# Moving the inverse transforms and norm of the next row block into the h stage, with block 0 by pairs and two VectorE orders changed

## The chip, the cores and the metric

The kernel runs on one core of one Trainium2 chip. The metric is the device time in microseconds (us), taken over several runs. One run of each kernel was also profiled; the span of a profile is the time from its first to its last instruction and is about 2 us shorter than the same run's time. Engines are named as in the profile: PE is TensorE, PEld its weight loads, DVE VectorE, ACT ScalarE, POOL GpSimd, SP SyncE. The granted clock is the share of TensorE's full clock that the profile records, 1.00 at full speed. L851 is a line of the kernel; the changed kernel has other line numbers than the one before for the same operation (the transposed input's product h is L833 before and L851 after, the row products og L858 and L878, the w2T scaling L619 and L622).

## The reference, cut to what matters

The reference is the forward pass of a block with spectral mixing and an MLP, and all its gradients.

```python
sa, ca, ga, sb, cb, gb = silu(c) @ w_mod                # six rows of 512
h = layernorm(x) * (1 + ca) + sa
x = x + ga * irfft2(rfft2(h) * (w_r + 1j * w_i))        # 2048 x 512
h = layernorm(x) * (1 + cb) + sb
x = x + gb * (relu(h @ w1 + b1) ** 2 @ w2 + b2)         # F = 1792
...
out = x;  gradients of x, w_r, w_i, w1, b1, w2, b2, c, w_mod
```

The 2048 rows are 16 tiles of 128, in four row blocks of four tiles (b = 0 to 3, TB = 4, NB = 4). Every row block passes through the following stages:

- **g**: the last part of the inverse transform (psT, psY), the unfolding of y, x = x + ga y, and the norm n2rows.
- **h2r and h2T**: n2rows times (1 + cb) plus sb, written to DRAM, and read back transposed (blocks 1 to 3); block 0 is transposed on TensorE.
- **h**: h2T times w1, the relu and square, and gh, the gradient there.
- **o**: the output rows, h times w2.
- **gn**: the gradient rows, gh times w1T, and the gradient of the norm.

After the four blocks come grad_w1 beside the gradient's transforms, and grad_w2 beside the last row products.

## The kernel before

The loop over the blocks, and where g of the next block stands:

```python
        merge(stage_g(0))
        merge(stage_t(0))
        ...
        for b in range(NB):
            again0, again = f1_again(UT) if b == NB - 1 else ([], [])
            stage_h(b, again0)
            ...
            if b < NB - 1:
                merge(stage_o(b), stage_g(b + 1) + [lambda: None] * 3)
                ...
                merge(stage_gn(b, UT), parts + [lambda: None])
```

`merge` interleaves two lists in program order; a scheduler then decides each engine's final order by its own estimates, and every engine works through its order. `tc.issue_after(i)` holds what follows behind instruction i in that order. The end of the norm in stage g, where the round trip of the next block's h input begins:

```python
            def norm(j):
                ...                                      # x, statistics, n2rows of rows j, j + 1
                h2r = rows.tile([P, 2, D], BF16, name="h2r", bufs=1)
                nc.vector.tensor_tensor(h2r, n2b[b][:, j:j + 2, :], ...CB1_B..., op=ALU.mult)
                nc.vector.tensor_tensor(h2r, h2r, ...SB_B..., op=ALU.add)
                nc.sync.dma_start(h2_dram[:, t:t + 2, :], h2r)
                if b > 0:
                    nc.sync.dma_start(h2T[b][:, j:j + 2]..., h2_dram[:, t:t + 2, :]..., transpose=True)
```

The two scalings of w2T, all ahead of the first statistics, and the h stage with its column sums flushed in one place:

```python
    for h in range(2):
        for dc in range(4):
            wh = w2T[:, dc, h * F2:(h + 1) * F2]
            nc.vector.tensor_scalar(wh, wh, gb2x[:, dc:dc + 1], None, op0=ALU.mult)
    ...
        late, late_f1 = Delayed(2), Delayed(4)           # column sums, delayed by two
    ...
        def stage_h(b, extra):
            ...
            for fc in range(0, NFC, 2):                  # seven pairs
                ...
                if fc == 4:
                    late.flush()
                if fc >= 2 and extra:
                    extra.pop(0)()
```

## Time and profile before

| | before |
|---|---|
| time | 457.75 us median of 3 runs (457.12 to 461.03) |
| span of the profile, mean granted clock | 455.1 us, 0.966 |
| PE, DVE, ACT busy | 408.5, 362.0, 251.0 us (90%, 80%, 55%) |

The page's second part cuts the span into 40 slices of about 11.4 us. Each digit is a share in tenths, and 9 is 90% or more:

```profile
PE   2589899999699999995999599999999979997996
...
PEclk9979999999889999997999889999999999999899
```

The dips of PE in the 11th slice (from 114 us), the 19th (205 us) and the 23rd (250 us) are the hand-over of block 0 and the borders before the h stages of blocks 2 and 3, and the clock falls with them. A sum over one stretch runs from the last h product of block 0 to the first grad_w1 product, and holds nearly all of blocks 0 to 3 but the start. The columns are length; busy us and count of PE, weight loads, DVE, ACT and POOL; granted clock, DMA share, GB/s:

```profile
140.00:305.10 165.10, 153.35 (x758) 67.47 (x756) 127.90 (x270) 83.95 (x150) 0.14 (x2) 0.96 0.75 194
```

TensorE has 758 matmuls there, is idle for 165.10 - 153.35 = 11.75 us, and runs at a mean clock of 0.96.

### The profile page before, as it was taken

To read this page: it belongs to the slowest core of one execution; us is meant where nothing else is said; L and a number is where in the kernel's file an instruction comes from. 1 tells how busy PE (TensorE), PEld (TensorE's weight loads), DVE (VectorE), ACT (ScalarE), POOL (GpSimd) and SP (SyncE) were. 2 spreads that over 40 slices of the span, in tenths; PEclk is the share of its full clock that TensorE was granted. 3 is DMA by queue.
4 is the path that set the end of the run, shared out by engine and by line. 5 is a ranking of instruction groups with operands and counts; after the bars stand their busy time and mean duration, and the time that the engine had idled before them with its cause. 6 is when DMAs were issued, how large, how long until landed. Compare 5 with 4: busy or idle time off the path is not lost.

```text
span 455.1 us, 7052 instructions
## 1 busy us (share of the span) xinstructions
PE 408.5 (90%) x2375; PEld 198.9 (44%) x2375; DVE 362.0 (80%) x864; ACT 251.0 (55%) x470; POOL 12.6 (3%) x64
## 2 busy tenths in 40 slices
PE   2589899999699999995999599999999979997996
PEld 0134455664344434442444234445555655443332
DVE  6379889987997487895679879891965995998996
ACT  4247877658874176355724376645453648364531
POOL 6011000000000000000000000000000000000000
PEclk9979999999889999997999889999999999999899
DMA  9995679998579359749933899598799559999995
GB/s 241 235 269 143 177 281 279 286 290 211 158 283 254 100 117 269 231 119 185 307 130 93 191 232 302 207 226 228 205 268 337 157 155 295 254 229 280 250 224 188
DMA packets 149738, 101.09 MB, mean 222 GB/s; under 512 B 98753, under 2 KB 135494, under 8 KB 149062
## 3 DMA queue, kind: packets, MB, share of 16 engines
q1 hardware_dynamic: 149138, 100.12, 81.8%
q10 hardware_dynamic: 564, 0.53, 0.4%
q8 instruction: 18, 0.29, 0.3%
q14 instruction: 18, 0.15, 0.1%
HBM read 35.44 MB, written 41.60 MB: 169 GB/s over the span
## 4 chain that ended last, share of the span: by engine, by line
PE 46%; DVE 29%; DMA 10%; SPq 5%; ACT 5%; issue 4%; POOL 1%; DVEq 0%; ACTq 0%; POOLq 0%
PE mm L833 11%; PE og L858 8%; PE mm L1053 7%; PE mm L684 6%; PE mm L1122 3%; PE psC L303 2%; PE psG L341 2%; DMA h2T<-h_dram 2%; DMA w2T<-in_B_w_dram 2%; DMA n<-n_dram 2%; DVE gab L687 2%; DVE l_st L784 2%; SPq L1117 2%; SPq L563 1%; DVE gm_junk L465 1%
## 5 line engine op out<-in xcount | busy, mean ns | idle before, releaser
L684 PE MATMUL mm<-gT,w2T 128*128 128x512 bf16 x224 | 60.1, 398 | 9.4 <-DVE gab L687 8.9
L833 PE MATMUL mm<-h2T,w 128*128 128x512 bf16 x224 | 59.8, 412 | 5.1 <-DMA h2T<-h_dram 4.5
L1122 PE MATMUL mm<-g_sb,hn 128*128 128x512 bf16 x224 | 51.7, 385 | 2.5 <-DVE gw L1125 2.5
L1053 PE MATMUL mm<-gab,h_sb 128*128 128x448 bf16 x256 | 51.7, 352 | 0.6 <-ACT gw L1057 0.6
L858 PE MATMUL og<-w1T,gab 128*128 128x512 bf16 x224 | 50.9, 379 | 0.4 <-DVE o L923 0.4
L858 PE MATMUL og<-w,h 128*128 128x512 bf16 x224 | 51.1, 379 | 0.0
L835 ACT ACTIVATE r<-mm,b1col 128x512 bf16<-128x512 f32 x56 | 37.7, 686 | 18.8 <-PE mm L833 13.9
L833 PEld LDWEIGHTS <-w 128*128 128x128 bf16 x224 | 22.7, 104 | 37.1 <-issue 18.6
L684 PEld LDWEIGHTS <-w2T 128*128 128x128 bf16 x224 | 21.7, 101 | 33.1 <-issue 16.0
L1053 PEld LDWEIGHTS <-h_sb 128*128 128x128 bf16 x256 | 24.7, 98 | 22.5 <-issue 2.1
L1122 PEld LDWEIGHTS <-hn 128*128 128x128 bf16 x224 | 21.3, 99 | 28.8 <-issue 5.4
L858 PEld LDWEIGHTS <-h 128*128 128x128 bf16 x224 | 21.8, 98 | 25.7
L858 PEld LDWEIGHTS <-gab 128*128 128x128 bf16 x224 | 21.5, 98 | 25.8 <-issue 0.8
L837 DVE TENSOR_TENSOR h<-r 128x1024 bf16<-128x1024 bf16 x28 | 19.3, 689 | 13.9 <-ACT r L835 13.8
L687 DVE CAST gab<-mm 128x512 bf16<-128x512 f32 x28 | 19.1, 681 | 4.8 <-PE mm L684 4.8
L689 ACT CAST gab<-mm 128x512 bf16<-128x512 f32 x28 | 16.5, 590 | 9.4 <-PE mm L684 9.2
L871 ACT CAST G<-og 128x512 bf16<-128x512 f32 x16 | 9.2, 578 | 22.5 <-PE og L858 22.5
L1202 ACT ACTIVATE gs<-gn,inv 128x512 bf16<-128x512 bf16 x16 | 11.4, 716 | 18.4 <-DVE gn L1200 18.4
L1057 ACT CAST gw<-mm 128x448 bf16<-128x448 f32 x16 | 8.7, 541 | 22.1 <-PE mm L1053 15.5
L372 ACT ACTIVATE Tsb<-psT 128x512 bf16<-128x512 f32 x32 | 18.5, 604 | 3.3 <-PE psT L370 3.3
L413 DVE TENSOR_TENSOR p<-Z,G 128x1028 bf16<-128x1028 bf16 x8 | 5.6, 696 | 17.6 <-ACT gw L1057 9.2
L465 DVE SCALAR_TENSOR_TENSOR gm_junk<-wmc,onef,gmbc 128x512 bf16<-128x512 bf16 x24 | 17.9, 745 | 1.9 <-DMA wmc<-in_w_mod_dram 1.0
(286 smaller groups left out, 749.1 us busy)
## 6 DMA issues: line engine op xcount, KB each, us to landing
h_dram<-h SPq DMA_DIRECT2D x28, 256.0 KB, 3.0
gh_dram<-gab SPq DMA_DIRECT2D x28, 256.0 KB, 3.1
w<-in_B_w_dram SPq DMA_DIRECT2D x2, 1792.0 KB, 8.4
wmc<-in_w_mod_dram SPq DMA_DIRECT2D x12, 256.0 KB, 4.9
out_dram<-gwm SPq DMA_DIRECT2D x12, 256.0 KB, 3.4
wz_dram<-Z SPq DMA_DIRECT2D x8, 258.0 KB, 2.3
xs_dram<-Xs SPq DMA_DIRECT2D x8, 258.0 KB, 4.6
Z<-wz_dram SPq DMA_DIRECT2D x8, 258.0 KB, 4.4
```

The lines of the kernel that those rows point to most:

```text
L372: nc.scalar.activation(Tsb, ps, AF.Copy, scale=EF_S)
L465: nc.vector.scalar_tensor_tensor(out=junk, in0=wmc[:, i, :], scalar=K["onef"], in1=gmbc, op0=ALU.mult, op1=ALU.mult, accum_out=self.gsc[:, ...
L684: nc.tensor.matmul(ps, lhsT=w2T[:, dc, fc * P:(fc + 1) * P], rhs=gT[b][:, :, dc, :], start=(dc == 0), stop=(dc == 3))
L687: nc.vector.tensor_copy(out=gaT[b][:, fc, :], in_=ps)
L689: nc.scalar.copy(out=gaT[b][:, fc, :], in_=ps)
L833: nc.tensor.matmul(ps, lhsT=w1[:, dc, (fc + i) * P:(fc + i + 1) * P], rhs=h2T[b][:, :, dc, :], start=(dc == 0), stop=(dc == 3))
L835: nc.scalar.activation(r[:, i, :], ps, AF.Relu, bias=b1col[:, fc + i:fc + i + 1])
L837: nc.vector.tensor_tensor(h2, r, r, op=ALU.mult)
L858: nc.tensor.matmul(ps, lhsT=lhs(fc), rhs=rhs[:, fc, :], start=(fc == 0), stop=(fc == NFC - 1))
L1053: nc.tensor.matmul(ps[:, 0:W4], lhsT=h2_sb[:, t, dc * P:(dc + 1) * P], rhs=ghn[t // 4][:, t % 4, fs], start=(t == 0), stop=(t == NT - 1))
L1122: nc.tensor.matmul(ps, lhsT=hns[fc][:, t, :], rhs=g_sb[:, t, :], start=(t == 0), stop=(t == NT - 1))
L1202: nc.scalar.activation(gs[:, i, :], gn[:, i, :], AF.Copy, scale=inv1[:, t + i:t + i + 1], accum_out=rr[:, i, 0:1])
```

## The change

The intent is that the next block's h input is ready when TensorE is, that block 0 hands over sooner, and that VectorE does not stand in front of data that have not landed. In the prediction and below, A is the w2T order, B is block 0 and C is the move of g. The diff, cut to its core:

```diff
-    for h in range(2):                                   # A
+    def scale_w2(h):
         for dc in range(4):
             ...
+    scale_w2(0)
     for q in range(4):
         ...                                              # statistics of row quarter q
+        if q == 1:
+            with tc.issue_after(stats.ins):
+                scale_w2(1)
 ...
+    with tc.issue_after(last.ins):                       # B: table load ahead of time
+        nc.scalar.activation(warm, K["eps"], AF.Sqrt)
 ...
         def stage_g(b):
             def norm(j):
                 ...
-                h2r = ...; nc.sync.dma_start(h2_dram ...); transposed read of h2T
+        def stage_m(b):                                   # the same lines, on their own
+            return [lambda j=j: one(j) for j in (0, 2)]
 ...
         def stage_t(b):                                   # B: by pairs of rows
-            four rounds by column chunk: 4 transposes, 1 copy of 128 x 512
+            two rounds by row pair: 8 transposes, 4 copies of 128 x 256
 ...
-        late, late_f1 = Delayed(2), Delayed(4)            # C: column sums later
+        late, late_f1 = Delayed(4), Delayed(4)
-                if fc == 4:
-                    late.flush()
+                if fc in (2, 6):
+                    late.pop(2)
 ...
+                with tc.issue_after(K["gh"]):             # f1 scalings behind gh
                     nc.vector.tensor_tensor(v, v, ...GA_B..., op=ALU.mult)
 ...
-        merge(stage_g(0))
-        merge(stage_t(0))
+        g0, t0 = stage_g(0), stage_t(0)
+        merge(g0[0:3] + t0[0:1] + g0[3:5] + t0[1:2])
 ...
-            stage_h(b, again0)                            # C: g beside h
+                m = stage_m(0) if b == 0 else []
+                stage_h(b, m + stage_g(b + 1), 2 if b == 0 else 6)
-                merge(stage_o(b), stage_g(b + 1) + [lambda: None] * 3)
+                merge(stage_o(b), stage_m(b + 1) + [lambda: None] * 2)
```

The last argument of `stage_h` is the pair of products beside which the extra work begins.

More of the change, by code (lines that the diff above doesn't have):

```diff
@@ L153, in build_cf @@
     nc.vector.tensor_single_scalar(v, v, 1023, op=ALU.bitwise_and)
-    nc.scalar.activation(Cf, v, AF.Sin, scale=TWO_PI / 1024, bias=K["npi"])
+    last = nc.scalar.activation(Cf, v, AF.Sin, scale=TWO_PI / 1024, bias=K["npi"])
     nc.vector.tensor_scalar(Cf[:, 0:2, :], Cf[:, 0:2, :], efc[:, 2:3], None, op0=ALU.mult)
     K["Cf"] = Cf
+    warm = cpool.tile([P, 1], FP32, name="warm")
+    with tc.issue_after(last.ins):
+        nc.scalar.activation(warm, K["eps"], AF.Sqrt)
 def iotas_lf(tc, g):
@@ L626 @@
             with tc.issue_after(K["last"]):
-                nc.vector.bn_stats(st, x_sb[:, 4 * q + j, :])
+                stats = nc.vector.bn_stats(st, x_sb[:, 4 * q + j, :])
             nc.vector.bn_aggr(mv[:, j, :], st)
+        if q == 1:
+            with tc.issue_after(stats.ins):
+                scale_w2(1)
         i1 = inv1[:, 4 * q:4 * q + 4]
@@ L759, in stage_g @@
         def stage_g(b):
-            n2b[b] = rows.tile([P, TB, D], BF16, name="n2rows")
-            yb[b] = rows.tile([P, TB, D], BF16, name="y")
             Ts = {}
             def g2(j):
+                if j == 0:
+                    n2b[b] = rows.tile([P, TB, D], BF16, name="n2rows")
+                    yb[b] = rows.tile([P, TB, D], BF16, name="y")
                 Ts[j] = spec_g2(tc, K, CS, TB * b + j, rows, psR)
@@ L790, in norm, with one @@
                     nc.scalar.activation(n2b[b][:, j + i, :], x1[:, i, :], AF.Identity, bias=nb[:, i:i + 1], scale=inv2[:, t + i:t + i + 1])
-                if b > 0 and j == 0:
-                    h2T[b] = rows.tile([P, TB, 4, P], BF16, name="h2T", bufs=1)
+            return [lambda j=j: (j > 0 and g3(j - 1), j < TB and g2(j)) for j in range(TB + 1)]
+        def stage_m(b):
+            def one(j):
+                t = TB * b + j
                 h2r = rows.tile([P, 2, D], BF16, name="h2r", bufs=1)
@@ L797, in norm, with one @@
                 if b > 0:
+                    if j == 0:
+                        h2T[b] = rows.tile([P, TB, 4, P], BF16, name="h2T", bufs=1)
                     nc.sync.dma_start(h2T[b][:, j:j + 2].rearrange("p j c q -> p (j c) q"), h2_dram[:, t:t + 2, :].rearrange("p j d -> p (j d)"),
                                       transpose=True)
-            return [lambda j=j: (j > 0 and g3(j - 1), j < TB and g2(j)) for j in range(TB + 1)]
+            return [lambda j=j: one(j) for j in (0, 2)]
         def stage_t(b):
-            h2T[b] = rows.tile([P, TB, 4, P], BF16, name="h2T", bufs=1)
-            def one(dc):
-                pst = psR.tile([P, TB, P], BF16, name="pst2")
-                for j in range(TB):
-                    nc.tensor.transpose(pst[:, j, :], n2b[b][:, j, dc * P:(dc + 1) * P], K["ident"])
-                dst = h2T[b][:, :, dc, :]
-                if dc % 2 == 0:
-                    nc.vector.tensor_scalar(dst, pst, mcol[:, CB1_C, dc:dc + 1], mcol[:, SB_C, dc:dc + 1], op0=ALU.mult, op1=ALU.add)
-                else:
-                    nc.scalar.activation(dst, pst, AF.Identity, scale=mcol[:, CB1_C, dc:dc + 1], bias=mcol[:, SB_C, dc:dc + 1])
-            return [lambda dc=dc: one(dc) for dc in range(4)]
+            def one(j):
+                if j == 0:
+                    h2T[b] = rows.tile([P, TB, 4, P], BF16, name="h2T", bufs=1)
+                pst = psR.tile([P, 4, 2, P], BF16, name="pst2")
+                for dc in range(4):
+                    for i in range(2):
+                        nc.tensor.transpose(pst[:, dc, i, :], n2b[b][:, j + i, dc * P:(dc + 1) * P], K["ident"])
+                for dc in range(4):
+                    dst = h2T[b][:, j:j + 2, dc, :]
+                    if dc % 2 == 0:
+                        nc.vector.tensor_scalar(dst, pst[:, dc], mcol[:, CB1_C, dc:dc + 1], mcol[:, SB_C, dc:dc + 1], op0=ALU.mult, op1=ALU.add)
+                    else:
+                        nc.scalar.activation(dst, pst[:, dc], AF.Identity, scale=mcol[:, CB1_C, dc:dc + 1], bias=mcol[:, SB_C, dc:dc + 1])
+            return [lambda j=j: one(j) for j in (0, 2)]
         def ghn_part(b, fc):
@@ L823, in ghn_part, with stage_h @@
             nc.sync.dma_start(ghn[b][:, :, fc * P:(fc + 2) * P], gh_dram[fc * P:(fc + 2) * P, b * SB:(b + 1) * SB], transpose=True)
-        def stage_h(b, extra):
+        def stage_h(b, extra, first):
             sl = slice(b * SB, (b + 1) * SB)
@@ L840, in stage_h @@
                 gh = gaT[b][:, fc:fc + 2, :]
-                nc.vector.tensor_tensor(gh, r, gh, op=ALU.mult)
+                K["gh"] = nc.vector.tensor_tensor(gh, r, gh, op=ALU.mult).ins
                 nc.sync.dma_start(h_dram[fc:fc + 2, :, sl].rearrange("a p s -> p a s"), h2)
                 nc.sync.dma_start(gh_dram[fc * P:(fc + 2) * P, sl].rearrange("(a p) s -> p a s", p=P), gh)
-                if fc == 4:
-                    late.flush()
+                if fc in (2, 6):
+                    late.pop(2)
                 if fc in (4, 8):
                     late_f1.pop(2)
-                if fc >= 2 and extra:
+                if fc >= first and extra:
                     extra.pop(0)()
+            while extra:
+                extra.pop(0)()
         def sums(t):
@@ L948, in scale @@
                 v = gxl[t // TB][:, t % TB:t % TB + 2, :]
-                nc.vector.tensor_tensor(v, v, modb[:, GA_B, None, :].broadcast_to([P, 2, D]), op=ALU.mult)
+                with tc.issue_after(K["gh"]):
+                    nc.vector.tensor_tensor(v, v, modb[:, GA_B, None, :].broadcast_to([P, 2, D]), op=ALU.mult)
                 fold2(nc, v, fold1(nc, rows, v, 2, "yg", 1))
@@ L965 @@
             again0, again = f1_again(UT) if b == NB - 1 else ([], [])
-            stage_h(b, again0)
+            if b < NB - 1:
+                m = stage_m(0) if b == 0 else []
+                stage_h(b, m + stage_g(b + 1), 2 if b == 0 else 6)
+            else:
+                late.lag = 2
+                stage_h(b, again0, 2)
             parts = [lambda fc=fc: ghn_part(b - 1, fc) for fc in range(0, NFC, 2)] if b > 0 else []
             if b < NB - 1:
-                merge(stage_o(b), stage_g(b + 1) + [lambda: None] * 3)
+                merge(stage_o(b), stage_m(b + 1) + [lambda: None] * 2)
                 if b == NB - 2:
```

## The prediction

> **What bounds the kernel now.** I read the page's busy table first: PE is busy 90% of the 455.1 us span, DVE 80%, ACT 55%. A gain therefore has to come out of PE's idle time (455.1 - 408.5 = 46.6 us) and out of time when PE runs at a lower clock. Which stretches hold it? The table by stretches of time (columns: stretch, length, busy us and count of PE, weight loads, DVE, ACT, POOL, granted clock, DMA share, GB/s), cut at the stage borders:
>
> ```profile
> 0.00:24.00 24.00, 8.99 (x27) 3.11 (x28) 12.78 (x60) 8.86 (x15) 7.81 (x47) 0.96 1.01 242
> ...
> 118.30:128.80 10.50, 7.64 (x41) 4.16 (x41) 9.65 (x27) 7.65 (x15) 0.00 (x0) 0.67 0.87 300
> ...
> 204.20:227.60 23.40, 18.07 (x90) 7.46 (x88) 13.75 (x25) 14.60 (x25) 0.00 (x0) 0.85 1.04 247
> ...
> 253.30:259.80 6.50, 1.63 (x17) 1.00 (x17) 6.33 (x15) 1.85 (x5) 0.00 (x0) 0.84 1.05 203
> ```
>
> These are the start, the hand-over from block 0's norm to its h stage, and the borders before h of blocks 2 and 3. From 54 to 305 us the other stretches keep PE busy to 97% or more, but for 100.5 to 118.3 (92%). The change touches exactly these four. PE's own timeline (start, length, what, in brackets idle before and its releaser) at three of them:
>
> ```profile
> 23.77 2.29 PE L684 MATMUL mm<-gT,w2T 128*128 128x512 bf16 x5 [4.64 <-DVE gab L687]
> ...
> 211.51 3.57 PE L833 MATMUL mm<-h2T,w 128*128 128x512 bf16 x8 [3.46 <-DMA h2T<-h_dram]
> ...
> 259.80 6.89 PE L833 MATMUL mm<-h2T,w 128*128 128x512 bf16 x20 [1.07 <-DMA h2T<-h_dram]
> ```
>
> The first is a VectorE order: DVE stands in front of the second half of w2T, which has not landed, and PE's PSUM evictions queue behind it, as DVE's timeline says:
>
> ```profile
> 22.30 0.81 DVE L619 TENSOR_SCALAR w2T<-w2T,gb2x 128x896 bf16<-128x896 bf16 x2 [5.54 <-DMA w2T<-in_B_w_dram]
> ```
>
> The other two wait for h2T, the transposed input of the next h stage. The chain of waits, in order of time, shows what is behind it:
>
> ```profile
> 202.85 4.51 DMA h_dram<-h2r
> 207.38 4.09 DMA h2T<-h_dram
> ```
>
> The last h2r rows leave DVE at about 202.8, when gn (the second row product of a block) is almost over; the round trip through DRAM is another 8.6 us. DVE is late because the inverse transforms, unfold and norm of the next block start only beside the o rows: DVE is busy 21.82 of 25.0 us in 179.2 to 204.2, but idles 0.5 us per pair in much of the h stage before.
>
> **What the Trainium skill says.** "TensorE: Matmul & The Clock Gate", Part 1, What's actually happening: after an idle window of about 3.4 us the array runs at half rate until about 3.4 us of sustained work. The trace agrees: after the idle at 211.51, 8 matmuls take 3.57 us (446 ns each); later in the same stage 32 take 7.45 us (233 ns). "DMA: Bandwidth & Descriptors", Anatomy of one DMA: a fixed cost of about 2 us, mostly the write receipt, so a write and a dependent read are paid in series; here 4.51 and 4.09 us. "ScalarE: Activation LUTs", What ACT_TABLE_LOAD costs: 1283 ns; the trace has three loads of 1283 ns, the Sqrt one inside block 0's norm.
>
> **The change part by part.** Work is nearly conserved: the listed order of instructions has 4752 on PE in both, two more on DVE and three more on ACT (smaller transposed copies and a dummy Sqrt). It is a matter of order.
>
> (A) Second half of the w2T scaling after the statistics of row quarter 1. In the new DVE order four scalings, both folds of the first rows, a gab eviction and two statistics precede the next scaling. DVE should wait some 2 us there instead of 5.54, and PE should lose the 4.64 us idle and the second cold start (5 matmuls in 2.29 us at 23.77, 458 ns each). PE's new order puts 8 more of the gT,w2T matmuls before the end of the first forward transform (90 against 82). But from 66 to 100 us DMA share is 0.92 to 1.10 and PE is full, and block 0's x lands only at 109.9 behind the w1T transposes, so not all of it arrives at the end: 2.5 us of a possible 6.
>
> (B) Block 0 by pairs, h2r out of its norm, Sqrt table preloaded. Before, the fourth y is evicted at 109.9 and the last h2T copy ends at 127.36, after four serial rounds of transpose and copy through one PSUM buffer from 121.62 (5.7 us). By pairs only the second pair's 8 transposes (0.9 us) and four half-size copies on two engines (about 1 us) follow the last norm: about 3.5 us less. The table load (1.28 us) and two h2r products (2 x 0.6) also leave the chain in part, but DVE now has h2r, block 1's unfold and the copies there too (its order says so). h(0) effectively begins at 126.9 now (it ends at 139.83, and 56 matmuls at 1.85 us per 8 are 12.95 us). I expect about 123 to 124: 3 us.
>
> (C) g of the next block into h, only h2r and transposes beside o. Border before h(2): from 204.09 to 211.51 are 7.42 us, of which about 1.3 are real PE work (acc, psT, psY) that must go elsewhere: 6.1 lost. The cold clock adds 3.57 - 8 x 0.233 = 1.7. Together 7.8. Before h(3): 253.16 to 259.80 is 6.64, less 1.3, and 6.89 - 20 x 0.233 = 2.2 for the clock: 7.5. Removable: 15.3 us.
> What replaces it? I walk the new DVE order through h(1) and o(1) with the trace's durations (0.60 us per step of a 1024-column product, 1.28 per two statistics), with T the start of h(1). The first unfold and its products lie before the last gab; the second pair's statistics and unfold run between the o rows; the last h2r comes three products after the fourth o row, at T + 31 to 32. Write 2 to 4.5, transposed read 4.1 to 4.4: landing at T + 38 to 41. PE needs h 15.5 + o 12.6 + gn 12.1 = T + 40. So a wait of 0 to 1.5 us stays; I take 0.7 per border, 1.4.
> The price is paid in h. There ACT evicts 14 PSUM tiles (686 ns each) and PE, with two PSUM buffers, feels every other ACT operation: 8 matmuls take 1.85 us, not the 1.72 of the bare 215 ns pace. In h(2) the new ACT order puts two scalings v, two n2rows (about 3 us, formerly done in the gap), two Tsb and two y (0.6 each) among them: 9.8 + 3.1 + 2.2 = 15.1 us of ACT, so h(2) takes about 16 instead of 14 warm. Estimates of the price: h(1) 0.7, h(2) 2.0, h(3) 1.5, together 4.2.
> C nets 15.3 - 1.4 - 4.2 = 9.7 us.
>
> The delay of the last f1 scalings behind gh is a guard for h(3) and I give it nothing alone. From 305 us on both orders are almost the same: 0.
>
> Sum: 2.5 + 3.0 + 9.7 = 15.2; 457.75 - 15.2 = 442.5 us.
>
> **The rivals.** (1) DVE becomes the bound. Per block it has about 37 us of work against a new period of 41 to 42 (47.3 now between h(1) and h(2)), in fixed order beside a full PE. For: its order places statistics behind o rows, so it waits for PE and PE later waits for it. Against: the h stage has real DVE idle (0.5 us before most h squares). It would eat about half of C: 447 to 449. (2) A new wait for h2T in the same place, since the transposes queue behind other DMA (SyncE issues in order, one transpose about 1.25 us): if each border keeps 3 to 4 us, PE also restarts cold: 448 to 451. For: the last landing is still within 2 us of need in my walk. Against: DMA share in the o and gn stretch is only 0.37 to 0.64. (3) The start gain is hidden: x and w1T set the begin of block 0, A gives 0 and B half: 446. (4) Better than thought: A passes fully (5 to 6 us), ACT's extra work fits into gaps: 435 to 437.
>
> **Range and chances.** A spans 0 to 5.5, B 1 to 4.5, C 5 to 14; not all at one end together: 435.5 to 450. Faster by 2% means below 448.6, a gain of 9.2 us, which C nearly gives alone: 0.87. Within 2% needs rival 1 or 2 together with 3: 0.12. Slower needs a stall that nothing here shows: 0.01.
>
> **What would show it.** A right: no PE gap of 4 us between 19 and 24, and the w2T scaling waits under 3 us. B: h(0) ends near 136 less A's share; no Sqrt table load in the norm. C: idle before the first h matmul of blocks 2 and 3 under 1.5 us, granted clock near 1.0 there, and h stages of 15 to 17 us. Wrong if those h stages take 18 us or more (ACT or DVE bound), if h2T still ends several us of idle, or if the gain reappears as waits after 305 us.

## The result, and the profile after

Ratios here are taken over the fast runs of both kernels in the same rounds, so they are not quite the ratio of the medians quoted.

| | before | after |
|---|---|---|
| time, median | 459.39 us (457.12 to 462.0, 4 runs) | 442.03 us (439.62 to 445.23, 4 runs) |
| ratio, 95% interval | | 0.9625 (0.9538 to 0.9712): faster |
| span of the profile, clock | 455.1 us, 0.966 | 440.3 us, 0.975 |
| PE, DVE, ACT busy | 408.5, 362.0, 251.0 us | 402.3, 361.0, 250.5 us |

The two slice lines of the kernel after (a slice is now 11.0 us):

```profile
PE   2888999999599999999999999999999799994996
...
PEclk9999999999789999999999999999999999997899
```

The dips in the middle are gone in both lines; the one of block 0 and two in the last quarter are still there. The table by stretches for the kernel after, cut at the places that answer the four of the prediction:

```profile
0.00:24.00 24.00, 12.59 (x49) 5.26 (x50) 16.27 (x68) 11.75 (x24) 8.14 (x48) 1.00 1.01 240
118.30:128.80 10.50, 9.49 (x41) 4.42 (x41) 8.96 (x22) 6.91 (x13) 0.00 (x0) 0.69 0.47 173
194.00:217.00 23.00, 22.89 (x121) 10.02 (x122) 18.12 (x38) 18.81 (x35) 0.00 (x0) 1.00 0.85 230
241.00:259.60 18.60, 17.90 (x103) 7.97 (x104) 18.57 (x42) 13.53 (x25) 0.14 (x2) 1.00 1.03 219
```

The start does 49 matmuls instead of 27 in its first 24 us. The border before h of block 2 lies inside 194 to 217, where PE is now busy 22.89 of 23.00 us at full clock, against 18.07 of 23.40 at 0.85. The h stage of block 3, the last line, shows VectorE busy for 18.57 of 18.60 us, and PE for 17.90. The three PE lines of the prediction, in the timeline of the kernel after:

```profile
23.49 2.83 PE L692 MATMUL mm<-gT,w2T 128*128 128x512 bf16 x12 [0.77 <-DVE gab L695]
...
200.72 1.46 PE L851 MATMUL mm<-h2T,w 128*128 128x512 bf16 x6
...
240.97 1.89 PE L851 MATMUL mm<-h2T,w 128*128 128x512 bf16 x8
```

The idle time in front of the h products of blocks 2 and 3 is gone, and they run at 1.46 / 6 = 0.243 and 1.89 / 8 = 0.236 us each instead of 0.446 and 0.345. The VectorE line that waited 5.54 us for the second half of w2T reads now:

```profile
22.39 0.45 DVE L622 TENSOR_SCALAR w2T<-w2T,gb2x 128x896 bf16<-128x896 bf16 x1 [1.09 <-DMA w2T<-in_B_w_dram]
```

Cutting each profile at three places, the end of the first inverse stage g1, the end of h of block 0 and the first grad_w1 product, gives one row per kernel. All twelve experiments are listed with the two first profiles. Stretches are differences of rounded ends and can be off by 0.1:

| kernel | g1 ends | h(0) begins | h(0) ends | from there to grad_w1 | grad_w1 to the end | span |
|---|---|---|---|---|---|---|
| before | 100.1 | 123.3 | 140.0 | 165.1 | 150.0 | 455.1 |
| after | 97.9 | 121.2 | 136.5 | 149.9 | 153.9 | 440.3 |
| control (after, again) | 98.0 | 122.6 | 138.2 | 149.9 | 151.5 | 439.6 |
| A undone | 99.1 | 122.8 | 138.2 | 149.9 | 151.6 | 439.7 |
| B undone | 98.0 | 122.0 | 138.7 | 149.8 | 151.9 | 440.4 |
| C undone | 97.4 | 121.8 | 137.1 | 165.5 | 151.6 | 454.2 |
| x first | 98.2 | 121.4 | 137.5 | 149.9 | 151.8 | 439.2 |
| x first, A undone | 98.8 | 122.5 | 137.8 | 149.9 | 153.7 | 441.5 |
| GpSimd loads | 97.0 | 122.1 | 136.7 | 149.9 | 156.5 | 443.1 |
| before with GpSimd loads | 98.8 | 122.7 | 139.3 | 164.3 | 156.0 | 459.6 |
| h2r held back | 97.8 | 121.8 | 137.1 | 155.9 | 151.2 | 444.2 |
| g earlier in h | 98.0 | 121.5 | 136.6 | 149.3 | 151.5 | 437.4 |
| column sums as before | 97.7 | 122.0 | 137.4 | 152.9 | 151.0 | 441.3 |
| no guard on f1 | 97.7 | 123.3 | 138.9 | 150.7 | 151.0 | 440.6 |

The table already tells where the time went. The column "from there to grad_w1" falls by 15.2 us and repeats within 0.1 us wherever C and the guard on f1 are untouched. The columns before and after it scatter by 2 to 3 us between kernels that do not differ there. In the two first profiles the last column seems to give 3.9 us back (150.0 against 153.9). This was the first thing to doubt.

### The profile page after: what moved, and what is told of

It reads as the page before. It is cut to its first block, busy times and chain, and to the rows that moved or that the text cites. A ratio compares the mean times of both kernels' runs of the same rounds, so it can differ in the third digit from the quotient of the medians.

```text
span 440.3 us, 7034 instructions
## 1 busy us (share of the span) xinstructions
PE 402.3 (91%) x2353; PEld 196.9 (45%) x2375; DVE 361.0 (82%) x866; ACT 250.5 (57%) x473; POOL 12.6 (3%) x64
## 4 chain that ended last, share of the span: by engine, by line
PE 32%; DVE 32%; DMA 14%; SPq 11%; ACT 5%; issue 4%; POOL 1%; DVEq 0%; ACTq 0%; POOLq 0%
PE og L878 10%; PE mm L851 9%; PE mm L1148 4%; PE mm L692 3%; SPq L981 3%; DMA n<-n_dram 3%; DMA LGb<-LG_dram 2%; DVE gm_junk L468 2%; DMA w2T<-in_B_w_dram 2%; DVE l_st L793 2%; SPq L1143 2%; SPq L566 2%; DMA gT<-in_grad_out_dram 2%; DVE jk L1233 1%; DVE gab L695 1%
## 5 line engine op out<-in xcount | busy, mean ns | idle before, releaser
L692 PE MATMUL mm<-gT,w2T 128*128 128x512 bf16 x224 | 56.6, 385 | 4.5 <-DVE gab L695 3.3
L851 PE MATMUL mm<-h2T,w 128*128 128x512 bf16 x224 | 54.7, 388 | 1.3 <-ACT r L853 1.1
L1148 PE MATMUL mm<-g_sb,hn 128*128 128x512 bf16 x217 | 52.6, 393 | 3.6 <-DVE gw L1151 3.2
L878 PE MATMUL og<-w1T,gab 128*128 128x512 bf16 x217 | 49.9, 379 | 1.1 <-DVE o L943 0.7
L878 PE MATMUL og<-w,h 128*128 128x512 bf16 x217 | 49.0, 379 | 0.2
L851 PEld LDWEIGHTS <-w 128*128 128x128 bf16 x224 | 21.6, 99 | 30.6 <-issue 9.2
L891 ACT CAST G<-og 128x512 bf16<-128x512 f32 x16 | 9.2, 580 | 25.4 <-PE og L878 14.4
L1228 ACT ACTIVATE gs<-gn,inv 128x512 bf16<-128x512 bf16 x16 | 11.4, 715 | 17.6 <-DVE gn L1226 17.6
L697 ACT CAST gab<-mm 128x512 bf16<-128x512 f32 x28 | 16.5, 590 | 5.5 <-PE mm L692 5.4
L468 DVE SCALAR_TENSOR_TENSOR gm_junk<-wmc,onef,gmbc 128x512 bf16<-128x512 bf16 x24 | 17.9, 745 | 1.8 <-DMA wmc<-in_w_mod_dram 0.9
```

Of the source, the lines that this page charges most:

```text
L468: nc.vector.scalar_tensor_tensor(out=junk, in0=wmc[:, i, :], scalar=K["onef"], in1=gmbc, op0=ALU.mult, op1=ALU.mult, accum_out=self.gsc[:, ...
L692: nc.tensor.matmul(ps, lhsT=w2T[:, dc, fc * P:(fc + 1) * P], rhs=gT[b][:, :, dc, :], start=(dc == 0), stop=(dc == 3))
L697: nc.scalar.copy(out=gaT[b][:, fc, :], in_=ps)
L851: nc.tensor.matmul(ps, lhsT=w1[:, dc, (fc + i) * P:(fc + i + 1) * P], rhs=h2T[b][:, :, dc, :], start=(dc == 0), stop=(dc == 3))
L878: nc.tensor.matmul(ps, lhsT=lhs(fc), rhs=rhs[:, fc, :], start=(fc == 0), stop=(fc == NFC - 1))
L1148: nc.tensor.matmul(ps, lhsT=hns[fc][:, t, :], rhs=g_sb[:, t, :], start=(t == 0), stop=(t == NT - 1))
```

## The experiments

Four kernels each were run on one chip with five rounds, beside the kernel before. The control's ratio to the kernel before was 0.9637; differences to it on another chip are taken through the ratio, one thousandth of which is about 0.46 us. All runs were correct. Runs count as slow when they are 1.5% above the fastest of their kernel; that happened to three of six runs of "B undone" and of "GpSimd loads". On one core, with a scatter of 5 us and more, it may only cut the upper half off, so for these two the means of all six runs are given too.

### 1. The changed kernel again

No edit.

> The changed kernel once more, unedited, as the control that the next three runs are held against on the same chip, and to see whether its tail is always longer. Theory (the delay of the tail is a property of the new schedule): the stretch from the first grad_w1 matmul to the end of the profile is again 153 to 155 us, against 150 us in the kernel before. Rival (it is scatter of one execution): 149 to 152 us. Time 440 to 444 us under both.

Measured: 440.54 us median (438.63 to 443.45), ratio 0.9637 (0.9590 to 0.9683). The last stretch was 151.5 us, so the rival holds: 153.9 was scatter. The last stage waits for n, the reloaded rows, in the kernel before and in both profiles of the changed one. VectorE's waits in it (us in total, times, longest), first the kernel before:

```profile
DVE q L1203 <- DMA n<-n_dram: 3.3, 3, 1.8
```

Then the control:

```profile
DVE q L1229 <- DMA n<-n_dram: 4.9, 3, 3.2
```

The wait is 1.6 us longer in the control, although the source of this stage is the same, and it varies from 4.1 to 5.8 us over the profiles of the changed kernel and its runs without A and B.

### 2. Part A undone

```diff
     scale_w2(0)
+    scale_w2(1)
 ...
-        if q == 1:
-            with tc.issue_after(stats.ins):
-                scale_w2(1)
```

> Only part A undone: the second half of the w2T scaling is put back directly behind the first half. Theory (A is worth what the traces show, 2.2 us at the end of the first inverse stage, and hands it on whole): 2 to 3 us slower than the control, with PE idle 4 to 5 us near 20 us again. Rival 1 (x of block 0, which lands behind the w1T transposes, hides it): within 1 us of the control although the PE gap is back. Rival 2 (A passes on more than the prediction took): 4 to 6 us slower.

Measured: 441.63 us median (440.05 to 443.97), ratio 0.9659 (0.9624 to 0.9693); the mean is 441.7 against the control's 440.9, so 0.9 us slower, inside the intervals. The idle time at the start is back:

```profile
23.96 2.29 PE L690 MATMUL mm<-gT,w2T 128*128 128x512 bf16 x5 [4.27 <-DVE gab L693]
```

Yet h of block 0 begins at 122.8 instead of 122.6 and ends at 138.2 in both. Rival 1 holds in its outcome. Where did A's gain go? These are PE's totals between the end of g1 and the start of h of block 0, first in the control:

```profile
98.00:122.60 24.60, 18.84 (x115) 9.92 (x115) 18.56 (x44) 18.60 (x36) 0.00 (x0) 0.81 0.94 261
```

Then with A undone:

```profile
99.10:122.80 23.70, 21.02 (x136) 10.23 (x136) 20.10 (x47) 19.89 (x39) 0.00 (x0) 0.99 0.56 129
```

The gT,w2T products are a fixed supply, 224 in all, with which TensorE fills the time in which it would wait. With A more of them run at the start: 40 are left after g1 in the control and 62 with A undone (55 in the kernel before), and the supply ends at 110.9 us instead of 119.3. TensorE then has 21 matmuls fewer in this stretch, waits there (5.8 us idle against 2.7), and its clock is 0.81 instead of 0.99. But this idle time is not what sets the start of h of block 0. From the point where VectorE adds the first rows of block 0's x, VectorE and ScalarE work through one row pair after the other. In the eight profiles with A, B and the load of x in its place it takes 13.1 to 13.4 us from there to the first h product, although that product itself scatters from 121.2 to 123.3; with A undone it takes 14.4. So A gains 1 us on this way. In the control x is added at 109.16 us, after a wait of 1.34 us for its landing (the line stands under 5 and 6), and with A undone at 108.36, without a wait. That takes most of the 1 us back. All this is read from traces; experiments 5 and 6 put the part of x to the test.

### 3. Part B undone

```diff
-        merge(g0[0:3] + t0[0:1] + g0[3:5] + t0[1:2])
+        merge(stage_g(0))
+        merge(stage_t(0))                   # four rounds by column chunk, as before
 ...
+                if b == 0:
+                    stage_m(b)[j // 2]()     # h2r of block 0 in its norm
 ...
-        nc.scalar.activation(warm, K["eps"], AF.Sqrt)
```

> Only part B undone: block 0 in four rounds by column chunk, its h2r products inside its norm, no dummy Sqrt. Theory from the traces (B brought h of block 0 only 1.3 us nearer): 1 to 2 us slower than the control. Rival (the prediction's size): 3 us slower. A third way: B is worth more than 3 us because without it the products of block 0 also delay the h stage of block 0 that now carries block 1's norm.

Measured: 444.59 us median of six (438.61 to 446.06). Its three fast runs average 441.6, its six 443.5, against the control's 440.9: 0.7 or 2.7 us. In the profile h of block 0 ends at 138.7, 0.5 us later than in the control, although it begins 0.6 us earlier: a product needs one column chunk of all four rows, and by column chunks the first of them is there before the last (this is argued from the code, not shown). B is worth something between 0.5 and 2.7 us; what it is exactly stays open.

### 4. Part C undone

```diff
-                stage_h(b, m + stage_g(b + 1), 2 if b == 0 else 6)
+                stage_h(b, m, 2)
-                merge(stage_o(b), stage_m(b + 1) + [lambda: None] * 2)
+                merge(stage_o(b), stage_g(b + 1) + [lambda: None] * 3)
 ...                                          # h2r of blocks 1 to 3 in the norm again
 ...                                          # column sums Delayed(2), flush at fc == 4
```

> Only part C undone: unfold and norm of the next block stay beside the o rows with the h2r products in them, the column sums are delayed as before; A and B stay. Theory from the traces (C removes 15 us of waits and cold clock and costs about 1 us in the h stages): 13 to 16 us slower than the control, gaps of 3 us and 1 us before the h stages of blocks 2 and 3 with a clock near 0.85 there. Rival (the prediction's size): 9 to 10 us slower. If part of the gain is eaten in the tail by the earlier start itself, 10 to 12 us with a tail of 150 us.

Measured: 454.53 us median (452.89 to 456.12), ratio 0.9941 (0.9908 to 0.9975). The mean is 13.8 us above the control's. The stretch from h of block 0 to grad_w1 is 165.5 us, 15.6 more. The gap before h of block 2, in PE's timeline:

```profile
209.02 3.57 PE L853 MATMUL mm<-h2T,w 128*128 128x512 bf16 x8 [4.03 <-DMA h2T<-h_dram]
```

And the sum over the stretch, to be held against that of the kernel before (165.10, 153.35) above, in this run and then in the control:

```profile
137.10:302.60 165.50, 152.93 (x759) 67.47 (x757) 129.38 (x273) 84.36 (x151) 0.14 (x2) 0.96 0.75 195
```

```profile
138.20:288.10 149.90, 147.76 (x757) 65.51 (x756) 127.88 (x272) 82.51 (x149) 0.14 (x2) 1.00 0.83 216
```

It is the same work (757 to 759 matmuls; VectorE 127.9 us before and in the control). Against the kernel before, C takes 11.75 - 2.14 = 9.6 us of TensorE's idle time and 153.35 - 147.76 = 5.6 us of busy time, which is about what the clock makes (147.76 / 0.96 = 153.9). Only 2.14 us of idle time remain: from h of block 0 to grad_w1, TensorE is busy for 98.6% of the time, at full clock. The last stretch, 151.6 us with C undone, is no shorter than with it (151.5), so in this pair of profiles C gives nothing back there.

### 5 and 6. The load of x ahead of the w1T transposes, with and without A

```diff
-                nc.sync.dma_start(x1b[b], x_view[...])
+                K["x"] = nc.sync.dma_start(x1b[b], x_view[...]).ins
 ...
-        nc.sync.dma_start(w1T, B_w1, transpose=True)
+        with tc.issue_after(K["x"]):
+            nc.sync.dma_start(w1T, B_w1, transpose=True)
```

The reason is in SyncE's timeline of the control (start, length, what):

```profile
91.96 12.82 SPq L981 DMA_TRANSPOSE w1T<-in_B_w_dram  x1
105.01 0.86 SPq L761 DMA_DIRECT2D x<-in_A_x_dram  x2
```

and in VectorE's:

```profile
109.16 0.69 DVE L789 TENSOR_TENSOR x<-yg,x 128x1024 bf16<-128x1024 bf16 x1 [1.34 <-DMA x<-in_A_x_dram]
```

> The changed kernel with the load of block 0's x put ahead of the w1T transposes in SyncE's order (they come after it). In the control x landed at 109.1 us, behind 12.8 us of transposes, and VectorE waited 1.3 us for it, although y was ready. Theory (A's gain of 2.2 us is hidden by this landing): x lands before 103 us, no wait for it, h of block 0 starts at 120 to 121.5 us instead of 122.6, time 1 to 2 us below the control's 440.5. Rival (VectorE's and ScalarE's own order sets block 0): x lands early but h of block 0 starts at 122 to 123 as in the control, and the time is the same.

> The run before with part A undone as well. With A undone alone, h of block 0 started at 122.8 us against 122.6 in the control, so A was worth nothing there. Theory (x hid A): with x out of the way A is worth its 1 to 2 us, so h of block 0 starts at 122.5 to 123 here against 120 to 121.5 with A. Rival (the evictions of the gT,w2T products, of which A moves eight to an earlier place, share VectorE with block 0 and A is worth nothing either way): both start within 0.5 us of each other.

Measured: 441.06 us median, ratio 0.9633 (0.9597 to 0.9670), with A; 442.14, ratio 0.9641 (0.9606 to 0.9675), without. Nobody waits for x any more. h of block 0 begins at 121.4 with A and 122.5 without, 1.1 us apart, as the first theory has it. But the ends of that stage are 137.5 and 137.8, and the times are 0.6 us apart in the mean: most of the lead is lost again within the h stage (16.1 us against 15.3). The trace with A shows where. The write of block 0's first h2r, issued at 117.21, takes about 6 us to land; VectorE waits for its buffer between two copies of h2T, and TensorE for the second copy:

```profile
123.26 0.69 DVE L808 TENSOR_TENSOR h2r<-n2rows,modb 128x1024 bf16<-128x1024 bf16 x1 [1.27 <-DMA h_dram<-h2r]
124.33 1.19 PE L851 MATMUL mm<-h2T,w 128*128 128x512 bf16 x4 [1.06 <-DVE h2T L830]
```

Neither the run without A nor the control has this wait. So the landing of x did hide A at the start of h of block 0, and the edit put another wait of about the same size in its place; what A is worth without either was not tested. By time the edit gains 0.2 us on the control, which is nothing.

### 7 and 8. The last stage's loads on GpSimd's queue

```diff
-            nc.sync.dma_start(rows3[t][0], n1_dram[:, t:t + 2, :])
-            nc.sync.dma_start(rows3[t][1], gx1_dram[:, t:t + 2, :])
+            nc.gpsimd.dma_start(rows3[t][0], n1_dram[:, t:t + 2, :])
+            nc.gpsimd.dma_start(rows3[t][1], gx1_dram[:, t:t + 2, :])
```

> The changed kernel with the loads of n1 and gx1 for the last row products issued from GpSimd's queue instead of SyncE's, where they stand behind the transposes of h that wait for TensorE to free a buffer. Theory (VectorE's waits for n in the last stage, 5.8 us in the changed kernel's first profile, come from SyncE's order and stretch the stage from the first grad_w2 matmul to the end to 69 to 71 us): waits for n under 1 us, this stage 66 to 67 us, time 1.5 to 4 us below the control's 440.5. Rival (the last stage is bound by VectorE's and TensorE's work and the waits are slack): stage and time as in the control within 1 us.

> The same edit made to the kernel before. If the change itself brought waits into the last stage (the reading of the two first profiles, 66.7 us before and 70.6 after), the edit gains nothing here (within 1 us of 457.3) and 2 to 4 us on the changed kernel. Rival (the last stage scatters by some us in both kernels for the same reason): it gains as much here as on the changed kernel.

Measured on the changed kernel: 444.15 us median of six (437.38 to 445.07), the three fast runs with ratio 0.9598 (0.9537 to 0.9659); the profiled run is one of the slow ones, so its times are not held against the others. On the kernel before: 460.06 us, ratio 1.0037 (1.0000 to 1.0074). The waits for n are gone in both profiles, and the stage is longer in both: from grad_w1 to the end 156.5 and 156.0 us, instead of 150 to 154. From the first grad_w2 product to the end of the profile, nearer to the stage that the expectation names, it is 75.1 us in the kernel before with this edit against 70.0 without; the changed kernel's slow run has 75.7, the control 72.4. Another wait stands in their place, here in the kernel before with this edit:

```profile
DVE gw L1125 <- DMA out_dram<-gw: 5.2, 1, 5.2
```

VectorE waits for the write of an earlier gw to free its buffer. The theory falls as stated: taking the waits for n away does not shorten the stage. On the kernel before the edit costs 1.7 us (459.8 against 458.1 in the means). On the changed kernel it is unclear: the three fast runs lie 1.8 us below the control by their ratio, the three slow ones are near 445 (means 439.7 of the three, 442.3 of all six). With a DMA share of 1.01 from 366.5 us on in the control, this suggests that the last stage waits for DMA as a whole and not for this one load; no run here tested that.

### 9. The last h2r held back

```diff
+                if b > 0:
+                    K["m1"] = m.pop()                     # second pair of blocks 2 and 3
 ...
-                nc.vector.tensor_tensor(q2, G, n2, op=ALU.mult)
+                q2_ = nc.vector.tensor_tensor(q2, G, n2, op=ALU.mult)
+                if j == 0 and "m1" in K:
+                    with tc.issue_after(q2_.ins):
+                        K.pop("m1")()
```

> The changed kernel with one thing held back: the second pair of h2r products of blocks 2 and 3 stands behind the first product q of gn instead of between the o rows; unfold, norm and everything else of C stay in the h stage. In the control the last h2r left VectorE at 194.0 us, the transposed read was issued at 196.4 and took 3.2, so it landed 2.8 us before h of block 2 began; q began at 197.2. Theory (C's gain is that the last h2T lands in time, nothing else): the read is issued some 5 us later, TensorE waits 2 to 3 us before h of blocks 2 and 3 again, at a lower clock there, time 4 to 8 us above the control's 440.5. Rival (C gains because VectorE's load is spread over the h stage): no more than 1 us.

Measured: 446.03 us median (444.23 to 449.62), ratio 0.9741 (0.9701 to 0.9782): 4.8 us above the control. The stretch is 155.9 us, 6.0 longer. The waits before the h products of blocks 2 and 3:

```profile
204.96 1.24 PE L851 MATMUL mm<-h2T,w 128*128 128x512 bf16 x5 [1.29 <-DMA h2T<-h_dram]
...
248.99 3.26 PE L851 MATMUL mm<-h2T,w 128*128 128x512 bf16 x14 [2.75 <-DMA h2T<-h_dram]
```

The theory's figures hold for the time and for the second border; the first waits less than said. The h2T waits are 4.0 of the 6.6 us of added idle time; another 1.4 us is a psT that now waits for ScalarE in front of the first border, and 1.4 a row product that waits longer for VectorE's o. The clock did not fall: 14 products take 3.26 us, 0.233 each. So C needs the last h2T to land in time: late, it takes back 6.0 of the 15.6 us that the stretch gained. The rival as stated, 1 us at most, falls. That nothing else carries C, as the theory has it, does not follow: VectorE's spread load was left as it was here and not tested alone. The margin in the control (landing at 196.4 + 3.2 = 199.6, start of h at 202.4) is 2.8 us.

### 10. g earlier in the h stage

```diff
-                stage_h(b, m + stage_g(b + 1), 2 if b == 0 else 6)
+                stage_h(b, m + stage_g(b + 1), 2)
```

> The changed kernel with g of blocks 2 and 3 begun earlier in the h stage, beside the second pair of products instead of the fourth. In the traces TensorE is idle only 2 us between the end of h of block 0 and the first grad_w1 product, 149.9 us long in each run with C. Theory (TensorE bounds this stretch and puts other products where an eviction is late, so C has no price): the stretch stays 149.9 within 0.5 us and the time within 1 us of the control's 440.5. Rival (the prediction's price in the h stage, by ScalarE's evictions): 1 to 3 us longer.

Measured: 440.82 us median (439.15 to 444.43), ratio 0.9629 (0.9592 to 0.9666), the control within 0.4 us. The stretch is 149.3 us:

```profile
136.60:285.90 149.30, 147.62 (x758) 65.44 (x757) 127.82 (x272) 81.86 (x149) 0.14 (x2) 1.00 0.81 217
```

The theory holds, if with 0.6 us less instead of within 0.5: moving ScalarE's and VectorE's extra work to an earlier place in the h stage costs nothing.

### 11. The column sums as before

```diff
-        late, late_f1 = Delayed(4), Delayed(4)
+        late, late_f1 = Delayed(2), Delayed(4)
-                if fc in (2, 6):
-                    late.pop(2)
+                if fc == 4:
+                    late.flush()
```

> The changed kernel with the order of the column sums as before (two delayed, flushed at the third pair of h). In the kernel before a column sum waited 2.9 us for VectorE's last y at the border before h of block 3. Theory (the column sums are part of C's gain): a wait of 1 to 3 us returns at a border or in the h stage, time 1 to 3 us above the control. Rival (it came from VectorE's late g and goes with it): the stretch stays at 149.9 within 0.5 us.

Measured: 445.89 us median (441.68 to 446.84), ratio 0.9708 (0.9669 to 0.9747): 3.2 us above the control. The stretch is 152.9 us, 3.0 longer:

```profile
137.40:290.30 152.90, 149.15 (x757) 65.81 (x756) 128.51 (x272) 81.56 (x149) 0.14 (x2) 1.00 0.81 212
```

The size is what the theory said, and its wait is not: the column sums wait only 0.6 us in all for y. The rest is spread: 1.6 us more idle time and 1.4 us more busy time than in the control. How it comes about was not followed further. The order of the column sums is a part of C that the prediction had given no value of its own.

### 12. The f1 scalings without their guard

```diff
-                with tc.issue_after(K["gh"]):
-                    nc.vector.tensor_tensor(v, v, ...GA_B..., op=ALU.mult)
+                nc.vector.tensor_tensor(v, v, ...GA_B..., op=ALU.mult)
```

> The changed kernel without the rule that holds the last f1 scalings behind the product gh. Theory (as predicted, worth nothing by itself: TensorE fills h of block 3 with gn products, and VectorE is busy 18.3 of 18.3 us there either way): within 1 us of the control's 440.5 and the stretch to the first grad_w1 product 149.9 within 0.5. Rival (it guards h of block 3): 1 to 3 us longer.

Measured: 442.7 us median of 5 runs, ratio 0.9659 (0.9631 to 0.9688), about 1.0 us above the control with overlapping intervals; the stretch is 150.7 us, 0.8 longer. The guard is worth about 1 us, between the two theories; by the times alone it is not distinct from nothing.

No run beats the changed kernel clearly; "g earlier in h" and "x first" are level with it.

## Why the prediction was right or wrong

The time was right: 442.5 said, 442.03 measured, the control at 440.5. The gain said was 15.2 us, from 457.75; measured were 17.4 between the medians of the result, where the kernel before stood at 459.39, and 16.5 in the control's runs (457.4 - 440.9 in the means). The sum holds because two errors of opposite sign nearly cancel: A and B brought about 2.7 us together instead of 5.5, C 13.8 instead of 9.7. That they cancel is luck; that the borders before h of blocks 2 and 3 held most of the gain is not.

**A, said 2.5 us.** Its signs came as said: no gap of 4 us at the start, a w2T wait of 1.09 us. At the end of g1 it shows as 1.4 us (a mean of 97.8 over the ten profiles with A, 99.2 over the four without), and in the time as 0.9, not distinct from nothing. The step that failed is "not all of it arrives at the end: 2.5 us of a possible 6": less arrived. The prediction named the late x and still let 2.5 us pass it. In the traces VectorE adds x at 109.16 us in the control, after a wait for its landing, and at 108.36 with A undone. From there to the end of h of block 0 A does shorten the way: 28.1 to 29.0 us in the eight profiles with A and B, 29.8 in both without A. The supply of filling also shrank by more than the eight products counted: 40 are left after g1, against 55 in the kernel before. The third rival, "the start gain is hidden: x and w1T set the begin of block 0", was nearest. With x first A's lead at the start of h of block 0 was 1.1 us; how much of it the end would keep stays open.

**B, said 3.0 us.** The term was too large. A and B together bring the end of h of block 0 from 139.65 (two profiles) to 137.3 us on average over the eight profiles with both (136.5 to 138.9), 2.3 us instead of 5.5. The kernel with C undone, which keeps A and B, is 2.7 us faster than the one before. Of this B has 0.5 to 2.7. Counted from the addition of x, which takes out when x lands, h of block 0 ends after 29.5 us with B undone (one profile) and after 28.5 on average with both. The failing part is the claim that only 0.9 us of transposes and about 1 us of copies follow the last norm. From the end of the last n2rows to the end of the last h2T copy it was 5.8 us before and is 3.5 in the control, 2.2 us less instead of 3.5. The transposes took 0.93 as said, but VectorE works on other things between its two copies, here in the control:

```profile
122.12 0.41 DVE L830 TENSOR_SCALAR h2T<-pst,mcol 128x256 bf16<-128x256 bf16 x1 [0.82 <-PE pst L826]
122.45 0.69 DVE L793 BATCH_NORM_STATS2 l_st<-x 128x6 f32<-128x512 bf16 x1
123.05 0.68 DVE L808 TENSOR_TENSOR h2r<-n2rows,modb 128x1024 bf16<-128x1024 bf16 x1
123.64 0.41 DVE L830 TENSOR_SCALAR h2T<-pst,mcol 128x256 bf16<-128x256 bf16 x1
```

The prediction had said that VectorE "now has h2r, block 1's unfold and the copies there too", and gave that too little time.

**C, said 9.7 us net.** This is where the prediction was furthest off. The gross term, 15.3 us of idle time and cold clock at two borders, is what the whole of C brought: 15.2 us between the two first profiles, 15.6 between the control and "C undone", and 13.8 in the timed runs of these two. Its parts came out differently: 9.6 us of idle time and 5.6 of clock instead of 11.4 and 3.9. The prediction took about 1.3 us of TensorE work out of each border; the records show it busy for 2.1 and 1.6 us there. Both deductions were too large: 5.6 us in all, where the timed runs leave room for 1.5 and the stretch for none.

- The remaining h2T waits, 1.4 us, are 0. The walk had the last h2r at T + 31 to 32, T being the start of h of block 1; it left VectorE's order at T + 32.3. The error was in the durations: write and read were taken at 2 to 4.5 and 4.1 to 4.4 us from a busy border, and took 2.1 and 3.2, so that the landing came at T + 37.9 instead of T + 38 to 41.
- The price in the h stages, 4.2 us, is not seen. The step that failed is ScalarE's load: said to be 15.1 us in h of block 2, it was busy for 13.7 us there. Over the stretch TensorE was busy for 147.8 us at full clock, against 153.35 x 0.96 = 147.2 before, and idle for 2.1. The h stages took 14.8, 15.1 and 18.4 us, and by the prediction's own test the last one says "ACT or DVE bound". It is a bad test: between the h products of block 3 TensorE runs gn products, column sums and f1 rows that it would otherwise run later, and is busy for 17.9 of 18.4 us in the control. A stage that gets longer because it holds other work has not got slower. From the start of h of block 3 to grad_w1 it is 45.4 us in both first profiles, although the cold clock is gone there: TensorE has 17 more matmuls in it (258 against 241). Experiment 10 agrees.

Within C, the column sums carry about 3 us (experiment 11), and a last h2T that is late by a few us takes 5 to 6 back (experiment 9); what carries the rest was not separated. The first two rivals, VectorE as the bound and a new h2T wait, did not come; the second is 2.8 us away.

**From 305 us on, said 0.** The first profiles seemed to say that 3.9 us come back there. Eleven profiles of kernels with the changed kernel's last stage and no edit in it lie at 151.0 to 151.9 us but for two, 153.7 and 153.9; the only such profile of the kernel before is 150.0. So 1 to 2 us may be given back in the last stage, or nothing; one profile cannot tell, and this stays open. That C does it is not seen: the stretch was 151.6 us without C.

## What to carry to other kernels

Judge a move of work by the sum of the bounding engine's idle time and its clock over a whole stretch, not by the lengths of the stages: where a scheduler fills gaps, a stage gets longer by the filling, and that length is not a price. An early gain is handed on only if what sets the start of the next stage moves too: here a load landed at its own time, and A's gain ended in a wait for it. Work that fills idle time is a supply, and a gap closed with it early can open another one later. Before explaining a difference between two profiles, look at a second profile of the same kernel: here most of the 3.9 us in the last stage was scatter.

## What the Trainium skill lacked or had wrong

- "TensorE: Matmul & The Clock Gate", Part 1, What's actually happening, ties the half rate to an idle window of about 3.4 us. Before h of block 3 in the kernel before, no single wait was over 2.86 us (2.86, 1.08 and 1.07, with 1.6 us of small matmuls between them), and the next 20 products still took 6.89 us, 0.345 each; after one wait of 2.75 us in experiment 9 there was no loss (0.233). How much light work in a window still counts as idle is not said there.
- "DMA: Bandwidth & Descriptors", DMA Transpose (X-bar), gives constraints and no time on the issuing engine for a large load. Here one transposed load of w1T held SyncE's queue for 12.82 us, and the load of x behind it, which depends on nothing in it, landed late enough to cost VectorE 1.34 us.
- "DMA: Bandwidth & Descriptors", Issuing engine by pattern, calls loads from SyncE or ScalarE generally faster than GpSimd's. The kernel before agrees: n landed a median of 5.8 us after its issue from GpSimd's queue and 4.2 from SyncE's, gx1 7.9 and 4.4. The section does not say what else the runs show: the transfers left on SyncE's queue slowed too. The writes of gx went from 2.7 to 5.3 us and those of gw from 3.2 to 4.1, and the stage from grad_w1 to the end from 150.0 to 156.0 (one profile of each).
